# A fused recurrent attention and maxout layer on one core: another order of all its operations, 88 of them on other engines

## The chip, the cores and the metric

The kernel runs on one core of a Trainium2 chip. The metric is the device time of one execution in microseconds (us), as the median of several runs. The engines are named as in the profile: PE is TensorE (PEld its weight loads), DVE is VectorE, ACT is ScalarE, POOL is GpSimd, SP is SyncE, which issues all DMAs here.

## What is computed

The first half is a recurrence over 768 positions for 4 batches and 8 heads of 48 columns, the second a maxout layer on its output:

```python
for t in range(S):
    cur = einsum('bhd,bhe->bhde', u[None] * k[t], v[t])
    y[:, :, t] = einsum('bhd,bhde->bhe', r[t], state + cur)
    state = w[t][:, :, :, None] * state + einsum('bhd,bhe->bhde', k[t], v[t])
...
h1 = x @ w1                # x: y as 3072 tokens x 384;  w1, w2: 384 x 1024
h2 = x @ w2
out = maximum(h1, h2) @ w_out          # w_out: 1024 x 384
```

All inputs and the output are float32.

## The kernel before

The recurrence is worked in chunks of 256 positions, two positions to a partition (index i). Inside a chunk, decays are products of w, taken as prefix sums of logarithms; the products of r and k become matmuls, and a mask keeps the pairs of positions that may see each other. The 3 chunks of 4 batches are spread over eight *units*: units 0 to 3 are one batch of the first chunk each, unit 4 is batches 0 and 1 of the second chunk, unit 5 batches 2 and 3 of it, units 6 and 7 the same of the last chunk. Units of two batches have most operations once per batch (b) or twice as long. The maxout is folded: max(h1, h2) = relu(h1 - h2) + h2, so the kernel needs w1 - w2 (`wd_sb`), w_out (`wo_sb`) and w2 @ w_out (`wc_sb`).

Each operation has a short name with the unit first, then the batch or a group number. `@p`, `@d`, `@a` give the engine: POOL, DVE, ACT. What they do, with the line under which the profile shows them:

- `load.n.x` (L372): one of k, r, v, w of unit n from HBM into `lk`, `lr`, `lv`, `lw` (for some, into `wso`). `wload`, `woload`: the weights (`gT`, `wst` and `wso` as staging).
- `wp` (`lg`): product of two neighbouring w; `ln` (L387): its logarithm; `hi`, `lo` (L200, L202, L413): its split into two half-precision parts; `ex` (L398, or L395 and L396): prefix sum on PE; `mz` (L440, `MZ`): prefix sum plus the own term; `e0` (L436, in place in PSUM tile `G`) and `ie` (L460, `iE`): exponentials of the two.
- `rk`, `ru` (`rku`): r x k, times u; `dg` (L502): its row sums; `dd` (`gd`): a copy of them; `di` (L516): puts them on the diagonal of the mask tile `M`.
- `rw`, `kw`: r and k times the neighbouring w; `scale` (`rp`, `kp`): r and k times the exponentials; `vb` (`vp`): v in bfloat16.
- `tr` and `te` (L565, `RK`): transposes of rp and kp on PE and their copy; in units 5 to 7 `dt` (L582) instead, a transposing DMA.
- `kv` (L596): the state's update on PE; `st.n.0` (L612, `S_f`) and `st.n.1` (L615, `T`): added to the state; `sm` (`S_f<-T,W`): times the decay; `sb` (`S_b`): its copies in bfloat16.
- `sc` (L641): scores; `mk` (L650): masked copy of them from PSUM into `M`; `ya` (L688) and `yi` (L675): output from the scores and from the state, in one PSUM tile; `xe` (`xT`): its copy in bfloat16.
- `gt` (L706): x @ (w1 - w2), one of the groups of 512 columns; `rl` (L717 on ACT, L719 on DVE): relu; `op` (L725 and L729): output of one group of 128 tokens, 3 and 8 matmuls; `oe` (`osb`, `wb`): its copy; `os` (L743): its store.
- `hot` (L234): eight matmuls whose result is not used.

What sets the order is one list of these names, ORDER. Each engine does its operations in the order of that list, and SP issues the DMAs in that order too; an operation waits for its data and for the buffer that it writes. PSUM has four one-bank buffers `G` (prefix sums, transposes, `gt`, `op`, `hot`) and two two-bank buffers `Y` (`kv`, `sc`, and the output tile of `ya` and `yi`).

```python
for o in ORDER:
    o, _, e = o.partition("@")
    name, *a = o.split(".")
    a = [int(x) if x.isdigit() else x for x in a] + ([e] if e else [])
    if name in ops:
        ops[name](*a)
    else:
        unit[name](U[a[0]], *a[1:])
```

The engine letter chooses who does the operation. A product of 768 columns is done by DVE in one instruction and by POOL in two halves:

```python
def by_two(e, op, o, a, b):
    ...
    if e == "d" or n < 2 * HD:
        op(o, a, b)
    else:
        m = o.shape[1] // 2
        for g in (slice(0, m), slice(m, 2 * m)):
            op(o[:, g], a[:, g], b[:, g])
```

Of the kernel before, what the change touches and what calls it, by code (L numbers as in the profile page):

```python
# [54 lines left out]
load.0.w.1 load.0.w.0 wp.0.0@d hot.8.2 hot.8.3 load.2.w.0 zero.v.1@d wp.0.1@d mask ln.0.0 tri  # L55
zero.k.1@p load.1.w.0 ln.0.1 ex.0.0 load.1.r kw.0.0@d mz.0.0 wp.2.0@d rw.0.0@d load.1.k zero.o@p
load.0.v ie.0.0 uspread utake@a wp.1.0@d ex.0.1 ln.1.0 wload.1.0 mz.0.1 scale.0.1.0.0@p hot.8.0
zero.M.1@p ie.0.1 load.3.w.0 ru.0.0@d dg.0 rw.0.1@p kw.0.1@p scale.0.1.0.1@p wt.0.0 ex.1.0 we.0.0
e0.0.0 e0.0.1 wt.0.1 rk.1.0@d hot.8.5 vb.0.1@p load.2.r zero.v.2@d load.2.k load.1.v mz.1.0 ie.1.0
rw.1.0@d wt.1.0 wload.1.2 ln.2.0 ex.2.0 vb.0.0@a we.0.1 scale.0.0.0.0@d zero.k.0@d kv.0  # L60
scale.0.0.0.1@d tr.0.0.1 dd.0@p mz.2.0 woload.0 we.1.0 ru.1.0@p kw.1.0@p row.2 w2turn.0.0 e0.1.0
scale.1.0.0.0@d st.0.0@a tr.0.0.0 te.0.0.1@a sc.0.0.1.1 sc.0.0.0.1 w2turn.0.1 dg.1 te.0.0.0@a
w2take.0.0@a wload.0.2 load.2.v scale.1.1.0.0@d dd.1@p sb.0.0@a wp.3.0@p tr.1.0.1 e0.2.0 st.0.1
te.1.0.1@a rk.2.0@d zero.M.2@p di.0.0@d ie.2.0 zero.M.0@p rw.2.0@d hot.8.1 wload.1.1 ru.2.0@d
kw.2.0@p scale.2.1.0.0@p sc.0.0.1.0 sc.0.0.0.0 mk.0.0.1.0 vb.1.0@a hot.8.4 mk.0.0.0.0 mk.0.0.1.1
# [6 lines left out]
wocast.1@p gt.1.1 w2take.1.1@d woload.3 gt.0.0 rw.3.0@p woload.2 rl.0.0@a gt.1.2 load.4.w.0 rl.1.2@a
vb.2.0@p ru.3.0@p gt.0.3 rl.0.3@a ex.3.0 wocast.3@d wocast.2@a wocast.0@a rl.1.1@a di.2.0@d
sc.2.0.1.0 mk.2.0.1.0 gt.0.1 mz.3.0 e0.3.0 kw.3.0@p gt.1.0 dg.3 sc.2.0.0.0 kv.2 st.2.0@a rl.0.1@a
wp.4.0@d ie.3.0 scale.3.0.0.0@d mk.2.0.0.0 wfold.2 sb.2.1@d wfold.0 dd.3@p ln.4.0 load.3.v st.2.1
wfold.1 sb.2.0@d vb.3.0@a wl.2 hi.4@a lo.4@d ya.2.0.0.0 load.4.r rl.1.0@a di.3.0@d vb.3.1@a row.3
ya.2.0.1.0 wctake.1@a we.2 load.4.k wctake.2@a rk.4.0@d wctake.0@a scale.3.1.0.0@p tr.3.0.0 ex.4.0
mz.4.0 tr.3.0.1 ex.4.1 mz.4.1 te.3.0.0@a kv.3 te.3.0.1@a st.3.0@a yi.2.0 xe.2.0@d ie.4.0 op.1.1
oe.1.1@a st.3.1 load.4.v e0.4.0 sb.3.0@a ru.4.0@d gt.2.0 load.5.w.0 rl.2.0@a sc.3.0.0.0 sc.3.0.1.0
vb.4.1@a gt.2.2 op.1.0 rk.4.1@p rw.4.0@d kw.4.0@d scale.4.0.0.0@d scale.4.1.1.0@d scale.4.1.0.0@p  # L80
e0.4.1 rl.2.2@a scale.4.0.1.0@d op.0.1 sb.3.1@a row.4 oe.1.0@a tr.4.1.0 te.4.1.0@a tr.4.1.1 vb.4.0@a
op.0.0 sm.2@p wl.3 mk.3.0.0.0 ya.3.0.0.0 mk.3.0.1.0 ya.3.0.1.0 yi.3.0 oe.0.1@d ru.4.1@p wp.5.0@p
we.3 sm.3@p te.4.1.1@a gt.2.1 xe.3.0@a dg.4 ln.5.0 oe.0.0@d tr.4.0.1 te.4.0.1@a gt.3.0 rl.3.0@a
rl.2.1@a hi.5@a dd.4@d load.5.k kv.4 di.4.0@d sc.4.1.1.0 load.5.r load.5.v rk.5.0@d gt.2.3 rl.2.3@a
gt.3.2 tr.4.0.0 di.4.1@d te.4.0.0@a mk.4.1.1.0 gt.3.3 st.4.0 st.4.1 os.1.0 rl.3.3@a gt.3.1 rl.3.1@a
ru.5.0@p sc.4.1.0.0 rk.5.1@p sc.4.0.0.0 load.6.r sb.4.0@a vb.5.1@a op.2.1 load.6.w.0 lo.5@d wl.4
ex.5.0 mk.4.0.0.0 os.0.0 sb.4.1@a mk.4.1.0.0 oe.2.1@a mz.5.0 e0.5.0 rw.5.0@p ex.5.1 sc.4.0.1.0
load.6.k ru.5.1@p mz.5.1 ya.4.0.0.0 scale.5.0.0.0@d op.2.0 rl.3.2@a op.3.0 mk.4.0.1.0 e0.5.1 os.1.1
scale.5.0.1.0@d dt.5.0.0 ya.4.0.1.0 dt.5.0.1 kw.5.0@d row.5 oe.3.0@d os.3.0 wp.6.0@p ie.5.0
# [24 lines left out]
""".split()


# [681 lines left out]
```

## Time and profile before

| what | value |
|---|---|
| median of 3 runs | 146.66 us (146.49 to 146.94) |
| profiled execution | span 147.2 us, which is its own time here |
| mean granted PE clock | 0.987 |
| HBM read, written | 23.61 MB, 4.73 MB |

The page names time, engine, operation and the tiles written and read. In the list of waits a row has who waited, for whom, the total in us, the number of times and the longest. In a timeline a row has start, length, engine, line, operation, tiles, count, and in brackets the idle time of the engine just before and what ended it. In the groups, the first number after the bar is the busy time in us, the second the mean length in ns; then the idle time before. In the stretches, each engine has its busy time and number of instructions, PEclk is the granted share of PE's clock. The chain of work that ended last gives start, length and what stood on it.

### The profile page before, as it was taken

To read this page: it belongs to the slowest core of one execution; us is meant where nothing else is said; L and a number is where in the kernel's file an instruction comes from. 1 tells how busy PE (TensorE), PEld (TensorE's weight loads), DVE (VectorE), ACT (ScalarE), POOL (GpSimd) and SP (SyncE) were. 2 spreads that over 40 slices of the span, in tenths; PEclk is the share of its full clock that TensorE was granted. 3 is DMA by queue.
4 is the path that set the end of the run, shared out by engine and by line. 5 is a ranking of instruction groups with operands and counts; after the bars stand their busy time and mean duration, and the time that the engine had idled before them with its cause. 6 is when DMAs were issued, how large, how long until landed. Compare 5 with 4: busy or idle time off the path is not lost.

```text
span 147.2 us, 5536 instructions
## 1 busy us (share of the span) xinstructions
PE 136.8 (93%) x2403; PEld 84.2 (57%) x2404; DVE 116.9 (79%) x162; ACT 90.6 (62%) x164; POOL 90.0 (61%) x106
## 2 busy tenths in 40 slices
...
DVE  2489999999999999999999967399967589361511
...
PEclk9999999999999999999999999599999999999999
...
GB/s 104 323 325 357 335 401 394 366 286 304 214 241 277 212 226 282 312 255 174 205 192 177 292 251 207 141 138 291 250 136 78 131 271 20 0 210 62 4 56 157
DMA packets 71186, 31.84 MB, mean 216 GB/s; under 512 B 66293, under 2 KB 70390, under 8 KB 71162
## 3 DMA queue, kind: packets, MB, share of 16 engines
...
q14 instruction: 5, 0.04, 0.2%
HBM read 23.61 MB, written 4.73 MB: 193 GB/s over the span
## 4 chain that ended last, share of the span: by engine, by line
PE 41%; DVE 35%; issue 6%; POOL 6%; DMA 4%; ACT 3%; SPq 2%; DVEq 0%; POOLq 0%; ACTq 0%
PE G L729 12%; DVE M L650 9%; PE G L706 8%; PE G L234 7%; PE G L725 5%; DVE rp L176 4%; DMA lv<-in_v_dram 4%; DVE rku L176 3%; DVE dg L502 3%; POOL kp L180 3%; DVE M L516 3%; PE Y L688 2%; SPq L582 2%; POOL rku L180 2%; PE Y L675 2%
## 5 line engine op out<-in xcount | busy, mean ns | idle before, releaser
L729 PE MATMUL G<-wo_sb,gT 128*128 128x384 bf16 x192 | 35.8, 331 | 0.0
L706 PE MATMUL G<-xT,wd_sb 128*128 128x256 bf16 (+1 forms) x192 | 34.4, 326 | 0.7 <-ACT xT L168 0.6
L650 DVE CAST_PREDICATED M<-mask,Y 128x1024 bf16<-128x1024 int32 (+1 forms) x26 | 28.6, 1131 | 2.8 <-PE Y L641 1.9
L717 ACT ACTIVATE gT<-G 128x512 bf16<-128x512 f32 x43 | 24.5, 601 | 9.8 <-PE G L706 9.6
L729 PEld LDWEIGHTS <-gT 128*128 128x128 bf16 x192 | 19.0, 99 | 12.6 <-issue 0.3
L706 PEld LDWEIGHTS <-wd_sb 128*128 128x128 bf16 x192 | 17.9, 98 | 12.6 <-DVE wd_sb L176 0.6
L180 POOL TENSOR_TENSOR kp<-lk,iE 128x384 bf16<-128x384 f32 x16 | 17.1, 1096 | 9.3 <-DVE lk L176 4.2
L725 PE MATMUL G<-wc_sb,xT 128*128 128x384 bf16 x72 | 15.7, 327 | 0.0
L180 POOL TENSOR_TENSOR rku<-rku,u_b 128x384 f32<-128x384 f32 x14 | 14.5, 1053 | 2.0 <-DVE rku L176 2.0
L234 PE MATMUL G<-S_b 128*128 128x512 bf16 x47 | 13.6, 442 | 1.8 <-DVE S_b L263 1.8
L168 ACT COPY RK<-G 128x1024 bf16<-128x1024 bf16 x12 | 12.1, 1019 | 4.7 <-PE G L565 4.7
L168 ACT COPY osb<-G 128x384 f32<-128x384 f32 x7 | 3.4, 479 | 15.9 <-PE G L729 12.6
L180 POOL TENSOR_TENSOR rku<-lr,lk 128x384 f32<-128x384 f32 x8 | 10.9, 1393 | 2.5 <-DMA lk<-in_k_dram 1.7
L641 PE MATMUL Y<-RK 48*64 48x128 bf16 x384 | 9.0, 220 | 2.6 <-DVE M L650 2.4
L502 DVE TENSOR_REDUCE dg<-rku 128x16 f32<-128x768 f32 x12 | 11.0, 945 | 0.1
L641 PEld LDWEIGHTS <-RK 48*64 48x64 bf16 x384 | 6.2, 106 | 7.8 <-issue 6.7
L168 ACT CAST xT<-Y 128x768 bf16<-128x768 f32 x7 | 7.0, 1025 | 5.3 <-PE Y L675 4.0
L168 ACT CAST S_b<-S_f 64x768 bf16<-64x768 f32 (+1 forms) x14 | 8.7, 624 | 2.3 <-DVE S_f L612 2.0
L176 DVE TENSOR_TENSOR rp<-lr,G 128x768 bf16<-128x768 f32 (+2 forms) x11 | 8.8, 799 | 1.4 <-ACT G L436 1.4
L234 PEld LDWEIGHTS <-S_b 128*128 128x128 bf16 x48 | 5.1, 112 | 8.3 <-issue 3.3
L516 DVE TENSOR_TENSOR M<-identq,gd 128x512 int32<-128x512 int32 x12 | 9.2, 778 | 0.4 <-POOL gd L168 0.3
L168 DVE CAST xT<-Y 128x768 bf16<-128x768 f32 x5 | 5.1, 1017 | 5.5 <-PE Y L688 3.2
...
## 6 DMA issues: line engine op xcount, KB each, us to landing
...
```

The lines of the kernel that those rows point to most:

```text
L168: (nc.scalar.copy if e == "a" else nc.vector.tensor_copy if e == "d" else nc.gpsimd.tensor_copy)(o, i)
L176: op(o, a, b)
L180: op(o[:, g], a[:, g], b[:, g])
L234: nc.tensor.matmul(t, zz[:, 0:P], zz[:, 0:512], start=True, stop=True)
L502: nc.vector.reduce_sum(s.dg[:, b].rearrange("p i h -> p h i"), s.rku[:, b], axis=AX.X)
L516: (nc.vector if en == "d" else nc.gpsimd).tensor_tensor(out=o, in0=m, in1=g.unsqueeze(3).to_broadcast([P, 2, H, Q // 2]), op=ALU.bitwise_and)
L641: nc.tensor.matmul(t[q * Q:(q + 1) * Q, e, p * P:(p + 1) * P].rearrange("s (i g) -> s i g", i=2), s.kT[d, b, j, y * n + p, q, :], s.rT[d, ...
L650: nc.vector.copy_predicated(t[:, :, 2 * n * y:2 * n * (y + 1)].rearrange("s i (p e) g -> s p e i g", e=2), mask[:, j].bitcast(I32).unsquee ...
L706: nc.tensor.matmul(t[:, m * n * P:(m + 1) * n * P].rearrange("c (b t) -> c b t", t=P), wd_sb[:, ko, fo * P:(fo + 1) * P], s.xT[:, 0:n, ko, :],
L717: nc.scalar.activation(o, i, AF.Relu)
L725: nc.tensor.matmul(t[:, 0:HD], s.xT[:, a, ko, :], wc_sb[:, ko, :], start=(ko == 0), stop=False)
L729: nc.tensor.matmul(t[:, 0:HD], s.gT[:, c:c + P], wo_sb[:, f, :], start=False, stop=(f == FO - 1))
```

## The change

Only the list ORDER is changed. It has the same 652 operations in another order, and 88 of them have another engine letter: 27 from POOL to DVE, 19 from DVE to POOL, 20 from DVE to ACT, 15 from ACT to DVE, 5 from POOL to ACT, 2 from ACT to POOL. Of the loads, those of unit 0 begin with v instead of k.

```diff
 ORDER = """
-ident zero.s.1@p identq@a load.0.k load.0.r zero.m@p identb@p u zero.s.0@d zero.r@d rk.0.0@d
...
+zero.v.0@p ident zero.s.0@d zero.r@d hot.8.4 zero.s.1@p mask zero.o@p load.0.v vb.0.0@a zero.m@p
...
```

Three places of it, as the built programs have them. First DVE at the program's start, up to the first `mz` (`MZ`): before,

```order
L176 TENSOR_TENSOR rku<-lr,lk 128x768
L176 TENSOR_TENSOR lg<-lw 128x192
L254 MEMSET vp_77 128x8x2x8
L255 MEMSET vp_77 128x8x2x8
L176 TENSOR_TENSOR lg<-lw 128x192
L176 TENSOR_TENSOR lw<-lk,lw 128x4x48
L440 TENSOR_TENSOR MZ<-G,lg 128x4x48
```

and after the change:

```order
L176 TENSOR_TENSOR lg<-lw 128x192
L168 CAST identb<-osb 128x128
L168 COPY MZ<-osb 128x1
L440 TENSOR_TENSOR MZ<-G,lg 128x4x48 x2
L257 MEMSET M_82 128x512
L176 TENSOR_TENSOR lw<-lr,lw 128x4x48
```

The first `rku`, the memsets of `vp`, the second half of `lg` and the product of k and w have moved behind `MZ` or to POOL.

Second, DVE around unit 5's state sums and masks (`S_f` and `T` are `st.5.0` and `st.5.1`, the masked copies are `mk`): before,

```order
L650 COPY_PREDICATED M_80<-mask,Y 128x8x2x64
L612 TENSOR_TENSOR S_f<-Y,S_f 128x384
L650 COPY_PREDICATED M_80<-mask,Y 128x8x2x64
L615 TENSOR_TENSOR T<-Y,S_f 128x384
L440 TENSOR_TENSOR MZ<-G,lg 128x8x48 x2
L176 TENSOR_TENSOR lk<-lk,lw 128x16x48
L516 TENSOR_TENSOR M_81<-identq,gd 128x2x256
```

and after the change:

```order
L516 TENSOR_TENSOR M_81<-identq,gd 128x2x256
L176 TENSOR_TENSOR rku<-lr,lk 128x768
L612 TENSOR_TENSOR S_f<-Y,S_f 128x384
L176 TENSOR_TENSOR rku<-lr,lk 128x768
L615 TENSOR_TENSOR T<-Y,S_f 128x384
L650 COPY_PREDICATED M_80<-mask,Y 128x8x2x64 x2
L440 TENSOR_TENSOR MZ<-G,lg 128x8x48 x2
```

Both masked copies of batch 0 now stand behind `T`, with two products `rku` of unit 6 between. On PE, `sc.5.0.0.0` (the second score group of unit 5) now writes the `Y` buffer that `T` reads last; before, it wrote the one that the first masked copy reads.

Third, SP's DMAs around the transposes of unit 5 (`RK`) and the load of v of unit 6 (`lv`): before,

```order
L582 DMA_TRANSPOSE RK<-rp_73 128x8x128 x2
L472 DMA row<-MZ 1x1024
L743 DMA out_dram<-osb 128x384
L743 DMA out_dram<-wb 128x384
L582 DMA_TRANSPOSE RK<-kp_75 128x8x128 x2
L372 DMA lv<-in_v_dram 128x8x96 x2
```

and after the change:

```order
L582 DMA_TRANSPOSE RK<-kp_75 128x8x128
L472 DMA row<-MZ 1x1024
L743 DMA out_dram<-osb 128x384
L582 DMA_TRANSPOSE RK<-kp_75 128x8x128
L582 DMA_TRANSPOSE RK<-rp_73 128x8x128
L372 DMA lv<-in_v_dram 128x8x96 x2
```

The two `kp` that these transposes read were written by POOL before (`scale.5.1.0.0@p`, `scale.5.1.1.0@p`) and are written by DVE now; one store is no longer ahead of the load.

More of the change, by code (lines that the diff above doesn't have):

```diff
@@ L53 @@
 ORDER = """
-ident zero.s.1@p identq@a load.0.k load.0.r zero.m@p identb@p u zero.s.0@d zero.r@d rk.0.0@d
[L55 to L65, printed above, removed]
@@ L72 @@
[L72 to L83, printed above, removed]
@@ L84 @@
[L84 to L89, printed above, removed]
@@ new lines @@
+tr.1.0.1 sc.0.0.0.0 mz.2.0 ie.2.0 wload.0.0 kv.1 tr.1.0.0 load.3.r mk.0.0.0.0 st.1.0@a load.3.k
+row.2 st.1.1 te.1.0.1@a sb.1.0@a w2take.1.1@d sm.1@p di.1.0@d sc.0.0.0.1 mk.0.0.0.1 w2turn.0.0
+w2take.0.0@a e0.2.0 w2turn.0.1 w2turn.2.1 te.1.0.0@a w2take.0.1@a wocast.1@a wocast.2@a sc.0.0.1.1
+dg.2 ya.0.0.0.1 ya.0.0.1.0 rw.2.0@p yi.0.0 scale.2.0.0.0@d mk.0.0.1.1 w2turn.2.0 ya.0.0.0.0
+ya.0.0.1.1 xe.0.0@a w2take.2.0@a kw.2.0@p sc.1.0.1.0 wocast.0@p wfold.0 load.2.v wctake.0@a
+wdiff.1@d scale.2.1.0.0@d tr.2.0.0 mk.1.0.1.0 sc.1.0.0.0 sm.0@p mk.1.0.0.0 te.2.0.0@a sb.1.1@a
@@ new lines @@
+rl.0.2@a ya.2.0.0.0 di.3.0@d hi.4@a ya.2.0.1.0 xe.2.0@a scale.3.1.0.0@p kv.3 tr.3.0.0 oe.1.1@a
+tr.3.0.1 te.3.0.1@a lo.4@d op.1.0 st.3.0@d sb.3.1@a sb.3.0@a te.3.0.0@a st.3.1 ex.4.0 rk.4.0@d
+rk.4.1@d rw.4.0@d row.3 ex.4.1 mz.4.1 mz.4.0 oe.1.0@a load.4.v gt.2.3 sc.3.0.1.0 rl.2.3@a ie.4.0
+e0.4.0 e0.4.1 vb.4.0@a sc.3.0.0.0 gt.2.2 mk.3.0.1.0 mk.3.0.0.0 op.0.0 load.5.w.0 wl.3 yi.3.0
+ya.3.0.0.0 oe.0.0@a rl.2.2@a ya.3.0.1.0 load.5.r zero.v.2@p xe.3.0@a kw.4.0@p scale.4.1.1.0@d
+scale.4.0.1.0@d gt.2.1 rl.2.1@a scale.4.0.0.0@d gt.2.0 tr.4.1.1 ru.4.1@p tr.4.1.0 ru.4.0@d dg.4
@@ new lines @@
+dd.4@d gt.3.1 rl.2.0@a di.4.0@d op.2.1 scale.4.1.0.0@p te.4.1.1@a wl.2 vb.4.1@a kv.4 load.5.k we.2
+te.4.1.0@a sc.4.1.1.0 rl.3.1@a gt.3.0 op.0.1 sm.2@d we.3 wp.5.0@p ln.5.0 sm.3@p st.4.0 sb.4.0@a
+hi.5@a tr.4.0.0 rk.5.0@p ru.5.0@p di.4.1@d mk.4.1.1.0 st.4.1 lo.5@d sc.4.1.0.0 sb.4.1@a yi.4.1
+rl.3.0@a oe.2.1@a tr.4.0.1 te.4.0.0@a te.4.0.1@a ex.5.0 ya.4.1.1.0 mk.4.1.0.0 oe.0.1@d ya.4.1.0.0
+row.4 xe.4.1@a rk.5.1@d load.6.w.0 wp.6.0@d gt.3.2 gt.3.3 sc.4.0.0.0 sc.4.0.1.0 rl.3.2@a ex.5.1
+rl.3.3@a op.3.1 mz.5.0 ln.6.0 e0.5.0 wl.4 op.3.0 hi.6@a mk.4.0.0.0 load.5.v os.0.0 load.6.r mz.5.1
```

71 lines of the change are left out of this document (41 added, 30 removed).

## The prediction

> **What bounds the kernel now.** I read the page first: busy time, the slices, the chain that ended last.
>
> ```profile
> span 147.2 us, 5536 instructions
> PE 136.8 (93%) x2403; PEld 84.2 (57%) x2404; DVE 116.9 (79%) x162; ACT 90.6 (62%) x164; POOL 90.0 (61%) x106
> DVE  2489999999999999999999967399967589361511
> PEclk9999999999999999999999999599999999999999
> GB/s 104 323 325 357 335 401 394 366 286 304 214 241 277 212 226 282 312 255 174 205 192 177 292 251 207 141 138 291 250 136 78 131 271 20 0 210 62 4 56 157
> PE 41%; DVE 35%; issue 6%; POOL 6%; DMA 4%; ACT 3%; SPq 2%; DVEq 0%; POOLq 0%; ACTq 0%
> ```
>
> TensorE and VectorE share the chain: VectorE is full from slice 4 to slice 23 (of 3.68 us each) and has holes later; TensorE looks full all along. Its busy time contains pipelined ends, so the waits tell more. They are few, in the list of who waited for whom:
>
> ```profile
> PE Y L641 <- DVE M L650: 2.4, 3, 1.9
> PE G L234 <- DVE S_b L263: 1.8, 1, 1.8
> PE G L565 <- DVE rp L176: 0.8, 2, 0.5
> ```
>
> The second is the start of the program. What is left to win on TensorE is small, and most of it stands in one place, which TensorE's timeline and the stretches around it show:
>
> ```profile
> 79.89 0.42 PE L641 MATMUL Y<-RK 48*64 48x128 bf16 x16 [0.27 <-DMA RK<-kp]
> 81.77 0.42 PE L641 MATMUL Y<-RK 48*64 48x128 bf16 x16 [0.17 <-DVE M L650]
> 82.12 0.82 PE L706 MATMUL G<-xT,wd_sb 128*128 128x512 bf16 x3
> 87.29 1.46 PE L729 MATMUL G<-wo_sb,gT 128*128 128x384 bf16 x8
> 90.70 0.42 PE L641 MATMUL Y<-RK 48*64 48x128 bf16 x16 [1.94 <-DVE M L650]
> 91.54 2.16 PE L729 MATMUL G<-wo_sb,gT 128*128 128x384 bf16 x8
> 123.48 0.42 PE L641 MATMUL Y<-RK 48*64 48x128 bf16 x16 [0.24 <-DVE M L650]
> ...
> core 0: us, PE busy (x) PEld busy (x) DVE busy (x) ACT busy (x) POOL busy (x), PEclk, DMA share, GB/s
> 88.73:92.15 3.42, 1.48 (x24) 1.01 (x24) 2.90 (x3) 2.19 (x4) 3.42 (x5) 1.00 0.86 189
> 92.15:95.57 3.42, 3.42 (x100) 2.01 (x99) 1.13 (x3) 1.22 (x2) 1.85 (x2) 0.50 0.76 145
> 23.90:27.30 3.40, 2.50 (x59) 1.88 (x58) 3.40 (x6) 1.59 (x3) 3.32 (x4) 1.00 1.04 398
> ```
>
> TensorE stands still for 1.94 us at 88.76, is busy for only 1.48 us of the stretch of 3.42 us around that, and in the next 3.42 us it is granted half its clock: the same eight matmuls take 2.16 us instead of 1.46. So one late mask costs 1.94 us of waiting and 3.42 / 2 = 1.71 us of slow clock. The chain tells why it came late:
>
> ```profile
> 79.96 6.14 DMA lv<-in_v_dram
> 86.17 0.04 ACT vp L168
> 86.91 0.47 ACT G L436
> 88.55 0.95 DVE rp L176
> 89.51 1.15 DVE M L650
> ```
>
> The load of v of unit 6 was issued behind the transposes of kp (unit 5), which waited for GpSimd's scalings; ScalarE then stood at the cast of v, and behind it the exponential that VectorE's rp needs.
>
> **The change part by part.** 88 operations change engine: 27 go from GpSimd to VectorE, 19 back, 20 from VectorE to ScalarE, 15 back, 7 from either of GpSimd and ScalarE to the other. Priced by the groups by shape:
>
> ```profile
> L180 POOL TENSOR_TENSOR rku<-lr,lk 128x384 f32<-128x384 f32 x8 | 10.9, 1393 | 2.5 <-DMA lk<-in_k_dram 1.7 <-POOL gd L168 0.8
> L180 POOL TENSOR_TENSOR kp<-lk,iE 128x384 bf16<-128x384 f32 x16 | 17.1, 1096 | 9.3 <-DVE lk L176 4.2 <-ACT iE L460 3.9 <-issue 1.1
> L176 DVE TENSOR_TENSOR rku<-lr,lk 128x768 f32<-128x768 f32 x6 | 6.4, 1062 | 3.5 <-DMA lr<-in_r_dram 3.5
> L176 DVE TENSOR_TENSOR kp<-lk,iE 128x768 bf16<-128x768 f32 x2 | 2.2, 1108 | 0.1
> L168 DVE CAST xT<-Y 128x768 bf16<-128x768 f32 x5 | 5.1, 1017 | 5.5 <-PE Y L688 3.2 <-PE Y L675 2.3
> L168 ACT CAST xT<-Y 128x768 bf16<-128x768 f32 x7 | 7.0, 1025 | 5.3 <-PE Y L675 4.0 <-PE Y L688 1.3
> ```
>
> A full product costs GpSimd two halves (2 x 1.39 for rku, 2 x 1.10 for kp) and VectorE 1.06 and 1.11 once. Summed over all moves so, GpSimd loses 14.7 us, ScalarE gains 5.7, VectorE gains 2.9. GpSimd's saving is off the path except where kp was late. VectorE's gain is not, so I follow VectorE.
>
> *Its start.* Both kernels put 16 warm-up matmuls (L234) ahead of the first prefix sum, so VectorE's first MZ cannot start before the 8.25 us that it has now.
>
> ```profile
> 5.50 0.96 DVE L176 TENSOR_TENSOR rku<-lr,lk 128x768 f32<-128x768 f32 x1 [3.49 <-DMA lr<-in_r_dram]
> 8.25 0.36 DVE L440 TENSOR_TENSOR MZ<-G,lg 128x192 f32<-128x192 f32 x1 [0.48 <-PE G L398]
> 83.37 0.55 DVE L615 TENSOR_TENSOR T<-Y,S_f 128x384 f32<-128x384 f32 x1
> ```
>
> Between 5.50 and 8.25 VectorE now does six things (0.96 + 0.36 + 0.17 + 0.17 + 0.30 + 0.35 = 2.3 us by their rows); in the new order only one half of lg and the two small identity copies (0.6) are left there, since v, w and r are loaded ahead of k. So 1.7 us of work is pushed behind the first MZ. The loads themselves hide: k is then the fifth load, 1.54 MB into the queue, and by the GB/s row (104 and 323 over slices of 3.68 us) 1.57 MB have moved by 7.4 us; VectorE wants it at about 10.5.
>
> *Up to the second state sum of unit 5 (T, L615, 83.92 at its end).* From there the lists compare cleanly. Ahead of it come 27 operations from other engines, 19.7 us: five rku products or scalings (5.0), four kp scalings (4.3), wp of units 3 and 6 (1.9), the difference of weights (1.4), the rest small. Ahead of it go 26, 17.7 us: xT of three groups (3.0), wp, kw and rk of units 2, 4 and 5 (5.8), three osb copies (1.6) and so on. The two masks of unit 5, batch 0, are now behind it (2.4) and one diagonal ahead (0.7). Sum: +0.3. With 1.7 of the start, and 0.5 where the rp scaling of unit 5 meets an exponential that ScalarE reaches later (ScalarE has more to do from 50 us on), T ends at 83.9 + 2.5 = 86.4.
>
> Who waits for that: the score matmuls of unit 5, batch 0, second half, now take the PSUM buffer that T empties (now: the one that the first mask empties, the wait of 0.17 at 81.77). TensorE has done the same list of work at 82.9 in the trace (the end of the gate matmuls of 82.12). So it is 3.5 us late there, part in small waits for masks and buffers from 45 us on (about 1.5), the rest, some 2.0, in one wait at T.
>
> VectorE could also be earlier. Its operations stretch where GpSimd works beside it:
>
> ```profile
> L516 DVE TENSOR_TENSOR M<-identq,gd x12: 676/684/1497, 21.3 to 123.3; 128x512 int32<-128x512 int32 x12
> ```
>
> The same diagonal takes 0.68 or up to 1.50. [...] A sixth of GpSimd's work goes (14.7 of 90.0). The stretching in VectorE's rku group is 6.4 - 6 x 0.96 = 0.6 us, a tenth of it; on all of VectorE's 116.9 us that would be 11, of which a sixth is 1.8. So 0 to 1.8 us may come back, and I take 0.5, since the early products, where the lists stay mixed, keep their neighbours. The term is 3.5 - 0.5 = +3.0; its ends are +1.7 (all of the 1.8) and +4.5 (nothing comes back, and one more wait of 1 us like the one for the exponential).
>
> *After it.* Scalings of kp of unit 5 on VectorE let the transposes and the load of v go without GpSimd, and the exponential stands ahead of the cast of v on ScalarE. The wait of 1.94 goes, with it the slow clock, 1.71, and the 0.24 at 123.48 (those at 79.89 and 81.77 are inside the 82.9 above). What is late next is VectorE itself, which reaches unit 5's last mask with the same work ahead (92.9 against 93.0 us), 1.7 later less the 1.9 that it idles there now:
>
> ```profile
> 88.55 0.95 DVE L176 TENSOR_TENSOR rp<-lr,G 128x768 bf16<-128x768 f32 x1 [1.37 <-ACT G L436]
> 91.16 1.22 DVE L650 CAST_PREDICATED M<-mask,Y 128x1024 bf16<-128x1024 int32 x1 [0.52 <-PE Y L641]
> ```
>
> From there to the last mask it has 3.2 us more than now, but it idles more than that in this part (slices 30 to 33 read 6758: 1.4 slices or 5.2 us), so TensorE is the limit. Sum: -3.9, ends -2.2 (the clock is lost elsewhere) and -4.3 (the waits of 0.27 and 0.17 go as well).
>
> *The end.* Behind the last mask stand eight gate matmuls and five outputs as before, with relu split four to four instead of five to three; output is copied by ScalarE (0.48) instead of VectorE (0.56). -0.1, taken as 0; no load is left in the queue there.
>
> Sum: +3.0 - 3.9 = -0.9 on the profiled execution, whose own time is its span, 147.2; the median of the runs is 146.66, 0.5 lower. Forecast 145.8.
>
> **The rivals.**
> *The new wait also halves the clock (slower).* The stall at T is 2 us long and TensorE is busy before and after. If 1.94 us of it fall into one stretch of the clock's 3.42, the case in the trace repeats: +1.7, so 147.5. For: the row of 88.73, where 43% of busy time was too little. Against: 74% was enough at 23.90 (the clock stays at 9 in every slice but the 26th), and the stall may straddle two stretches. It decides from where the idle share of a stretch passes some point between 26% and 57%. [...]
>
> *VectorE keeps up.* If GpSimd's relief is the whole 1.8 and the pushed work of the start finds gaps later, T ends at about its old time; the small waits from 45 us on go with it. With +0.5 left of the term, 0.5 - 3.9 gives -3.4: 143.3. Against: no gap on VectorE above 0.5 us between 8.3 and 86 in which pushed work could hide.
>
> *More waits than a walk along two engines finds (slower).* ScalarE has 5.7 us more in its list. In the new order a copy of xT of unit 4 and the casts of v stand ahead of relus whose PSUM buffers TensorE wants next; one such wait is 0.5 to 1, three of them 2 to 3: 148.5 to 149.5. One copy of an output (group 4.0) now also shares its buffer with the store before it (4.2). For: casts of xT of 1.0 us at the head of that list. Against: ScalarE is 62% busy, so it catches up soon. It decides from where such a wait outlasts what TensorE has left in its four PSUM buffers, which no row shows.
>
> **How the numbers follow.** A change under 0.3%, 0.44 us, cannot be told from none here. Chances: the sum as it stands 0.38 (144.8 to 146.9, a quarter of it inside the 0.44, the rest faster), clock halved at the new place 0.27 (a quarter inside, the rest slower), VectorE keeps up 0.19, more waits 0.16. That is faster 0.28 + 0.19 = 0.47, same 0.10 + 0.07 = 0.17, slower 0.20 + 0.16 = 0.36. The range leaves out a tenth at each end: 143.0 to 149.3.
>
> **What would show it.** In the new profile: VectorE's first rku well behind 8 us (start); a wait of TensorE at L641 of about 2 us near 84 to 87, released by VectorE's L615 (the price); no wait of 1.94 and full clock between 88 and 96 (the gain); VectorE's holes after 97 smaller. Wrong would make it: waits of TensorE spread over 40 to 80 that ScalarE ends, a second stretch at 0.50, or no wait at L615.

## The result: 2.7% slower, and the profile after

The changed kernel takes 150.54 us (median of four runs, 149.89 to 151.59), the kernel before 146.80 beside it (146.49 to 147.06): a ratio of 1.0271, 95% interval 1.0223 to 1.0319. The forecast was 145.8.

A run's time is its span and 1.7 to 1.9 us more, so a median of 146.66 belongs to a span of about 144.9, and the profiled execution of before that the prediction read (span 147.2, clock 0.987) was of a rare kind: of 80 further runs of that kernel three had spans of 147.3 to 148.1 at a clock of 0.988, one 146.6, and the others 144.1 to 145.9.

The page of after, in the order of the lines shown of before (size, busy time, slices, DMA rates, chain):

```profile
span 148.2 us, 5530 instructions
PE 136.5 (92%) x2404; PEld 84.1 (57%) x2404; DVE 119.2 (80%) x165; ACT 96.1 (65%) x172; POOL 80.8 (55%) x92
DVE  2189999999999999999999899898599587545110
PEclk9999959999999999999999999999999999999999
GB/s 106 300 278 335 348 371 375 389 306 247 298 273 275 231 249 280 49 107 253 330 168 219 200 179 326 176 239 285 184 166 66 174 160 4 106 111 215 4 106 106
PE 45%; DVE 22%; SPq 13%; DMA 8%; POOL 5%; issue 4%; ACT 0%; DVEq 0%
```

GpSimd lost 9.2 us of its 90.0 (less than the priced 14.7), VectorE and ScalarE gained 2.3 and 5.5. VectorE is now full from slice 4 to slice 22, with two short dips behind. The loads have a hole of two slices near 60 us (49 and 107 GB/s). The half clock (0.50) has moved to 19.1 to 22.5 us. Little of its price shows, because the same kernel run again at full clock waits there instead (0.6 us for ScalarE and 0.8 for VectorE between 21.9 and 24.6 us). The list of TensorE's waits, as for before:

```profile
PE Y L688 <- issue: 1.8, 1, 1.8
PE Y L641 <- DMA RK<-kp: 0.9, 1, 0.9
PE G L565 <- DVE kp L176: 0.8, 1, 0.8
PE G L706 <- DVE rp L176: 0.7, 1, 0.7
```

The wait for masks (`PE Y L641 <- DVE M`) is gone. In its place stand many waits of less than 1 us, and one of 1.8 us at L688 with no releaser ("issue": nothing that the profile shows was waited for). Rows of the timelines of after, VectorE and then TensorE, at the places that the prediction named:

```profile
7.94 0.62 DVE L440 TENSOR_TENSOR MZ<-G,lg 128x192 f32<-128x192 f32 x2 [0.96 <-PE G L398]
11.02 0.90 DVE L176 TENSOR_TENSOR rku<-lr,lk 128x768 f32<-128x768 f32 x1
84.04 0.55 DVE L615 TENSOR_TENSOR T<-Y,S_f 128x384 f32<-128x384 f32 x1
...
84.55 0.64 PE L641 MATMUL Y<-RK 48*64 48x128 bf16 x32
108.29 0.94 PE L688 MATMUL Y<-M,vp 64*32 64x128 bf16 x84
111.06 0.57 PE L688 MATMUL Y<-M,vp 64*32 64x128 bf16 x44 [1.83 <-issue]
```

`T` ends at 84.59 and the scores behind it begin without a wait. At 108.3, 84 of the 128 matmuls of `ya` run; the other 44 follow 1.83 us later.

To see where the time went, I count TensorE's operations with the duration that each has when nothing holds it (0.65 us for a gate group, 1.80 for an output of 11 matmuls, 0.14 or 0.25 for a score group and so on: 122.4 us in all). What TensorE's time exceeds that sum by, up to the same amount of work, is lost time (us):

| work done | near | before, as predicted from | before, again | after | after, again |
|---|---|---|---|---|---|
| 20 | 29 us | 9.1 | 8.8 | 9.4 | 10.0 |
| 40 | 52 us | 11.9 | 11.7 | 12.7 | 13.2 |
| 60 | 75 us | 13.4 | 13.1 | 15.9 | 17.0 |
| 70 | 85 us | 14.7 | 14.4 | 16.5 | 17.5 |
| 85 | 103 us | 19.5 | 16.8 | 18.8 | 19.6 |
| 95 | 116 us | 20.1 | 17.4 | 21.8 | 22.5 |
| all | end | 21.7 | 19.0 | 22.6 | 23.3 |

The first column is some 0.3 too high throughout, since one warm-up matmul (L234) is missing from that trace (2403 records, 2404 in the others). Against the usual before, after loses 3.6 to 4.3 us: 0.6 to 1.2 by 29 us, 2.2 to 2.7 more by 75; it wins 0.8 to 1.1 back by 103, loses 2.3 to 2.4 more by 116, and wins 0.8 back by the end.

### The profile page after: what moved, and what is told of

Read it like the earlier page. It is cut to its first block, busy times and chain, and to the rows that moved or that the text cites. A ratio compares the mean times of both kernels' runs of the same rounds, so it can differ in the third digit from the quotient of the medians.

```text
span 148.2 us, 5530 instructions
## 1 busy us (share of the span) xinstructions
PE 136.5 (92%) x2404; PEld 84.1 (57%) x2404; DVE 119.2 (80%) x165; ACT 96.1 (65%) x172; POOL 80.8 (55%) x92
## 4 chain that ended last, share of the span: by engine, by line
PE 45%; DVE 22%; SPq 13%; DMA 8%; POOL 5%; issue 4%; ACT 0%; DVEq 0%
PE G L706 15%; PE G L729 14%; DVE M L650 7%; SPq L372 7%; PE G L725 6%; DMA lw<-in_w_dram 5%; SPq L285 4%; DMA RK<-kp 3%; POOL rku L180 3%; PE Y L688 3%; DVE rku L176 2%; DVE kp L176 2%; PE Y L641 2%; SPq L290 2%; PE Y L596 2%
## 5 line engine op out<-in xcount | busy, mean ns | idle before, releaser
L717 ACT ACTIVATE gT<-G 128x512 bf16<-128x512 f32 x41 | 23.5, 598 | 14.0 <-PE G L706 13.8
L706 PEld LDWEIGHTS <-wd_sb 128*128 128x128 bf16 x192 | 17.9, 98 | 13.1 <-issue 1.4
L180 POOL TENSOR_TENSOR rku<-rku,u_b 128x384 f32<-128x384 f32 x14 | 15.9, 1153 | 0.0
L234 PE MATMUL G<-S_b 128*128 128x512 bf16 x48 | 13.9, 447 | 1.8 <-DVE S_b L263 1.8
L168 ACT CAST xT<-Y 128x768 bf16<-128x768 f32 x10 | 10.3, 1029 | 3.7 <-PE Y L688 2.6
L168 ACT CAST vp<-lv 128x768 bf16<-128x768 f32 (+1 forms) x13 | 9.2, 707 | 4.6 <-DMA lv<-in_v_dram 4.6
L180 POOL TENSOR_TENSOR kp<-lk,iE 128x384 bf16<-128x384 f32 x10 | 11.2, 1144 | 0.1
L688 PE MATMUL Y<-M,vp 64*32 64x128 bf16 x768 | 9.1, 219 | 2.2 <-issue 1.8
L180 POOL TENSOR_TENSOR rku<-lr,lk 128x384 f32<-128x384 f32 x6 | 6.6, 1127 | 7.1 <-DVE gT L719 5.2
L234 PEld LDWEIGHTS <-S_b 128*128 128x128 bf16 x48 | 5.2, 114 | 8.9 <-issue 4.1
L641 PE MATMUL Y<-RK 48*64 48x128 bf16 x384 | 9.2, 223 | 1.0 <-DMA RK<-kp 0.9
L516 DVE TENSOR_TENSOR M<-identq,gd 128x512 int32<-128x512 int32 x12 | 9.7, 813 | 0.6 <-ACT gd L168 0.5
L688 PEld LDWEIGHTS <-vp 64*32 64x32 bf16 x768 | 7.2, 90 | 5.0 <-issue 4.4
L168 ACT COPY osb<-G 128x384 f32<-128x384 f32 x11 | 5.3, 478 | 7.2 <-PE G L729 7.1
L168 ACT CAST S_b<-S_f 64x192 bf16<-64x192 f32 (+1 forms) x16 | 9.4, 588 | 0.6 <-DVE S_f L612 0.4
```

Of the source, the lines that this page charges most:

```text
L168: (nc.scalar.copy if e == "a" else nc.vector.tensor_copy if e == "d" else nc.gpsimd.tensor_copy)(o, i)
L234: nc.tensor.matmul(t, zz[:, 0:P], zz[:, 0:512], start=True, stop=True)
L641: nc.tensor.matmul(t[q * Q:(q + 1) * Q, e, p * P:(p + 1) * P].rearrange("s (i g) -> s i g", i=2), s.kT[d, b, j, y * n + p, q, :], s.rT[d, ...
L688: nc.tensor.matmul(lhsT=s.vp[g, b, 2 * p + e, j, m * 32:(m + 1) * 32], rhs=s.M[b, j][g, :, 2 * p + e, :], **into(s, b, q, p * 96 + (e + m) ...
L706: nc.tensor.matmul(t[:, m * n * P:(m + 1) * n * P].rearrange("c (b t) -> c b t", t=P), wd_sb[:, ko, fo * P:(fo + 1) * P], s.xT[:, 0:n, ko, :],
L717: nc.scalar.activation(o, i, AF.Relu)
```

## The experiments

**The kernel before again.** Nothing is changed.

> The kernel before, unchanged, run and profiled again. Theory P (the profiled execution that the prediction read was longer than the usual ones, by a mask that came late once): span 144.5 to 145.5, time 146.5 to 147, no wait of TensorE of 1.9 us near 89 and full clock near 92. Theory Q (that execution was typical): the wait of 1.9 us and the half clock appear again, span about 147. If P holds, the 3.9 us that the prediction booked as a gain were never in the time to be beaten.

146.40 us, ten runs of 146.13 to 146.66. Its page:

```profile
span 144.7 us, 5537 instructions
PEclk9999999999999999999999999999999999999999
```

TensorE's timeline at the place of the wait:

```profile
89.66 0.42 PE L641 MATMUL Y<-RK 48*64 48x128 bf16 x16 [0.94 <-DVE M L650]
```

and the stretch around it:

```profile
88.42:91.84 3.42, 2.48 (x29) 1.35 (x27) 2.90 (x4) 1.45 (x4) 3.42 (x4) 1.00 1.04 217
```

The wait is 0.94 instead of 1.94, its stretch is 73% busy instead of 43%, and the clock stays. Theory P holds: TensorE's last matmul ends at 141.41 here and at 143.83 in the execution that was read, so 2.4 us of what was to be won was in that one execution and not in the time to be beaten.

**Order and letters apart.** Two kernels: the order of before with the 88 letters of after, and the order of after with the letters of before.

> The order of before with the 88 engine letters of after. If the loss of 3.7 us lies in the order (loads and transposes late in SP's queue, the start), this runs within 1 us of before: 146 to 148. If it lies in the letters (5.7 us more on ScalarE, 2.9 more on VectorE), it takes about what after takes, 149.5 to 151.5. If the letters fit only the order that was sought with them, it is slower than both, over 152.

> The order of after with the engine letters of before. Loss in the order: 149.5 to 151.5 as after. Loss in the letters: 146 to 148. Letters and order fitted to each other: over 152.

169.25 us (1.1496, 1.1432 to 1.156) and 168.27 (1.1496, 1.1444 to 1.1547). The third theory: letters and order fit only each other, and neither is good or bad by itself. The sum of prices by letter, with which the prediction began, says little about such a list.

**The changed kernel again.**

> The changed kernel, unchanged, run and profiled again. If its losses are built into the list (waits behind WL in SP's queue near 57 to 63, late transposes of unit 6 at 105, half clock near 21, a stop of 1.8 us without a releaser at 109), they stand at the same places again, span 148 to 149.8. If they are chance, other places show them and the span may come down to 146.

149.89 us (149.69 to 150.61), at full clock. The losses stand at the same places; rows of TensorE's timeline:

```profile
57.15 0.74 PE L688 MATMUL Y<-M,vp 64*32 64x128 bf16 x64 [0.68 <-DVE M L650]
59.38 0.82 PE L706 MATMUL G<-xT,wd_sb 128*128 128x256 bf16 x6 [0.72 <-DVE rp L176]
111.78 0.57 PE L688 MATMUL Y<-M,vp 64*32 64x128 bf16 x44 [1.75 <-issue]
```

So they are built into the list, and the stop without a releaser falls on the same matmul.

**An output between the small matmuls.**

```diff
-ya.6.1.1.0 ya.6.1.0.0 ya.6.0.0.0 ya.6.0.1.0 ... dt.7.0.0 op.5.3 op.5.2
+ya.6.1.1.0 ya.6.1.0.0 op.5.3 ya.6.0.0.0 ya.6.0.1.0 ... dt.7.0.0 op.5.2
```

> After, with one entry of the list moved: op.5.3 (11 matmuls of 128x384, 1.8 us) stands between ya.6.1.0.0 and ya.6.0.0.0 instead of four entries later. Theory I: the stop of 1.8 us of TensorE in ya.6.0.0.0 is a wait for its own instructions: a transfer of 16 KB on the instruction queue begins there at 109.5, and the dense ya matmuls (84 of them in 0.94 us) use up what is left before it lands; 11 slow matmuls bridge it. Then the stop goes and the run takes 1.5 to 2.0 us less than after: 148.0 to 148.5. Rival D: the stop is a wait for data (a masked copy, vp) that the trace does not name; then it stays behind op.5.3, and 0 to 0.3 us are won. Rival M: the stop moves to the next dense run (sc.7, ya.7): 0 won.

149.51 us (148.24 to 150.42; 1.0188, 1.0145 to 1.0232). In the trace the stop at `ya` is gone: the two halves of `ya` stand at 108.74 and 111.62 with `op.5.3` between (it waits 0.26 us for `osb`), and neither waits. But 0.5 us of a wait without a releaser appears at `kv.7`, 6 us on. The median is 0.4 below that of the repeated after, less than the spread of either. The place is confirmed, the price is not.

**Three operations off VectorE.**

```diff
-rk.4.1@d rw.3.0@d wctake.1@d
+rk.4.1@p rw.3.0@p wctake.1@a
```

> After, with rk.4.1 and rw.3.0 back from VectorE to GpSimd and wctake.1 from VectorE to ScalarE: 2.05 us less on VectorE ahead of the masks of unit 3. Theory V: TensorE's waits between 54 and 60 (0.85 at yi.3.0 for a mask, 0.90 at gt.2.1 for rp) come from VectorE's list, which has no gap from 9 to 86 us; they go, and 1.0 to 1.8 us are won: 148.1 to 148.9. Rival G: GpSimd's rk.4.1 (about 2.8 us) makes kw and kp of unit 4 late, the transposes wait instead, and the time stays within 0.4 of after or gets worse.

150.51 us (149.60 to 151.53; 1.0275, 1.0233 to 1.0317): the rival's time, but not its cause. The wait for the mask shrank from 0.68 to 0.35, the one for `rp` stayed (0.73), and the transposes of unit 4 behind it do not wait. What ate the gain in this trace is a new wait of 1.6 us for `xT` on VectorE, up to 98 us.

**Two buffers for WL.**

```diff
-s.WL = tile_of(s, [P, 2 * NP], F32, "WL", 1)[:, s.x * NP:(s.x + s.nb) * NP]
+s.WL = tile_of(s, [P, 2 * NP], F32, "WL", 2)[:, s.x * NP:(s.x + s.nb) * NP]
```

> After, with two buffers for WL instead of one, so that the load wl.4 need not wait for the exponentials we.2 and we.3, and SP does not stand at it between 56 and 63 us with the loads of units 5 and 6 behind it. Theory S: the hole in the loads (45 to 81 GB/s in two slices) makes v, r and k of units 5 to 7 late, and with them the last transposes and masks: 0.5 to 1.5 us won, 148.4 to 149.4. Rival H: the hole is hidden, because TensorE's waits grow by only 0.4 us between 60 and 82 us: within 0.3 of after, 149.6 to 150.2.

150.01 us (148.56 to 152.40; 1.0215, 1.0175 to 1.0256). The rates of slices 17 to 21 are 226, 283, 248, 80 and 84 instead of 49, 107, 253, 330 and 168: the hole is only moved, and the time did not change clear of the spread. The hole is hidden, as rival H said.

**An earlier copy on ScalarE.**

```diff
-vb.1.1@a ... ln.2.0 sb.0.0@a e0.1.0 we.1.0 w2take.1.0@a
+w2take.1.0@a vb.1.1@a ... ln.2.0 sb.0.0@a e0.1.0 we.1.0
```

> After, with w2take.1.0 (ScalarE's copy that frees a PSUM buffer) ahead of five other ScalarE operations instead of behind them, so that ex.2.0 at 22.6 need not wait 1.2 us for a buffer. If TensorE's waits at the start count by themselves, 0.8 to 1.2 us are won: 148.7 to 149.1. Rival: VectorE is full from 9 to 86 us, so TensorE, earlier here, waits the same time more at the masks of 54 to 60 us: 0 to 0.3 won, 149.6 to 149.9.

149.45 us (148.47 to 153.91; 1.0192, 1.0147 to 1.0237). The wait for ScalarE's buffer (0.63 us in the repeated after) is gone. Behind it TensorE waits longer for `rp` on VectorE (1.03 us in two waits instead of 0.83), and the mask wait of 57 us shrinks from 0.68 to 0.17. So in this trace TensorE is 0.6 us ahead of the repeated after at 28 us and 1.1 at 59, but level with the first trace of after (58.27 and 58.31 for the same gate matmuls). The median lies between the two expectations and within the spread: neither is shown.

**Halves of the two lists joined.** Before up to `yi.4.0` (73 us) and after behind it; the same with `op.5.3` between; and the opposite join.

> Two lists joined behind yi.4.0 (TensorE's last operation of unit 4's recurrence, at 73 us before): ahead of it order and letters of before, behind it those of after (op.3.1, ln.6.0, hi.6, we.4 stand at the seam). In the first part after loses about 2.7 us of TensorE's time to before (waits for VectorE from 14 to 30 and from 54 to 72 us), in the second it wins 2.0 (no wait for the masks of unit 5) and loses 2.0 (the stop of 1.8 in ya.6.0.0.0) and 0.4 (late transposes). Theory (the losses add, part by part): 146.5 + 0.4 = 146.6 to 147.4, if the stop is there with 1 to 1.8 us. Rival (the parts are tied by buffers and by VectorE's queue, as the order and the letters were): over 148.5.

> The joined list with op.5.3 between ya.6.1.0.0 and ya.6.0.0.0 too. Theory I (the stop is a wait for instructions in a dense run of small matmuls): 1.0 to 1.8 us less than the joined list without it, 145.0 to 146.2, so faster than before. Rival (the stop only changes place): the same as without it.

> The opposite join: after up to yi.4.0, before behind it. Theory (losses add): 146.5 + 2.7 = 148.5 to 149.8, with TensorE 2.5 to 3.5 us behind at yi.4.0 and full work from there. Rival (VectorE, late by the first part, finds slack behind it, since before has gaps there from 87 us on): 147 to 148.

149.63 us (148.02 to 149.85), 149.30 (147.95 to 150.27) and 151.97 (151.07 to 153.04); ratios 1.0202 (1.0159 to 1.0245), 1.018 (1.0136 to 1.0224), 1.0378 (1.0331 to 1.0424). The joins made waits of their own. In the first two ScalarE copies `xT` of unit 4 too late, and TensorE waits 2.2 us. What the prediction's first rival describes, half the clock behind such a wait, is in one of their two profiles. TensorE's timeline behind the wait in the first join:

```profile
77.61 2.75 PE L706 MATMUL G<-xT,wd_sb 128*128 128x512 bf16 x12 [2.22 <-ACT xT L168]
```

in the second:

```profile
77.53 4.44 PE L706 MATMUL G<-xT,wd_sb 128*128 128x512 bf16 x12 [2.21 <-ACT xT L168]
```

and the stretch behind the wait in the second (PEclk, third from the end, is 0.51; in the first join it is 1.00 throughout):

```profile
78.00:81.40 3.40, 3.40 (x10) 1.27 (x9) 2.28 (x3) 0.36 (x1) 0.00 (x0) 0.51 1.21 278
```

Behind the same wait at the same place the clock is halved in one execution and not in the other: the twelve matmuls take 4.44 us instead of 2.75. Of the first join's six runs the one at clock 1.00 has a span of 146.2, the five at 0.986 to 0.988 have 147.7 to 148.0, so 1.5 to 1.8 us more, near the 1.71 that the prediction gave one halved stretch. The second join's six runs divide in the same way: one at 0.999 with 146.2, five at 0.985 to 0.989 with 147.4 to 148.6. Where the clock falls was seen only in the one profile; that it is this place in the other runs is inferred from clock and span. What decides between the two is not shown.

The opposite join waits 2.4 us for masks (L641) and 1.2 us for `xT`. It is slower than the theory allowed, so the half of before does not run behind that of after as it does behind its own.

**Two copies and one scaling of before moved.**

```diff
-oe.3.0@d oe.2.0@d ... scale.6.0.0.0@d ... mk.5.1.0.0
+oe.3.0@a oe.2.0@a ... mk.5.1.0.0 scale.6.0.0.0@d
```

> Before, with the output copies oe.3.0 and oe.2.0 (0.55 us each) on ScalarE, which is idle from 70.3 to 73.7, instead of VectorE, and scale.6.0.0.0 behind mk.5.1.0.0 on VectorE. It asks whether before's own waits for the masks of unit 5 (0.68 and 1.10 us at 80 to 89) can be had without the new order. Theory: VectorE reaches those masks 1.0 to 2.0 us earlier and 0.9 to 1.7 us are won: 144.9 to 145.7. Rival: the next thing that VectorE needs (an exponential on ScalarE, behind the cast of v) is no earlier, and 0 to 0.4 are won.

145.43 us (eleven runs, 144.99 to 145.95; 0.9934, 0.9913 to 0.9956): 0.7% faster than before, little but clear of the spread. VectorE's timeline of the usual before, then the timelines of VectorE and of TensorE here:

```profile
88.39 1.22 DVE L650 CAST_PREDICATED M<-mask,Y 128x1024 bf16<-128x1024 int32 x1
...
87.24 1.21 DVE L650 CAST_PREDICATED M<-mask,Y 128x1024 bf16<-128x1024 int32 x1
...
88.82 0.42 PE L641 MATMUL Y<-RK 48*64 48x128 bf16 x16
```

The mask starts at 87.24 instead of 88.39, because the scaling that waited 0.36 us for ScalarE's exponential now stands behind it, and TensorE's wait of 0.94 is gone. The copies won nothing that shows: `T` ends at 84.06, and at 83.89 in before. What the usual runs have of the wait at 88 us goes, by these rows, when one operation is moved.

**The join mended.** `xe.4.0` ahead of `ln.6.0`; the same with `op.5.3` between; and with the two copies as well.

> The joined list (before up to yi.4.0, after behind it) with xe.4.0 ahead of ln.6.0 on ScalarE, so that TensorE need not wait 2.4 us at the seam for xT of unit 4, and the clock is not halved behind it (granted 0.986 to 0.988 in five of six runs of the first join). Theory (parts add): span 143.8 to 144.8, time 145.6 to 146.6, the stop in ya.6.0.0.0 still there. Rival (the seam's wait hid others on VectorE): over 147.5.

> The mended join with op.5.3 between ya.6.1.0.0 and ya.6.0.0.0. Theory I (the stop is a wait for instructions): 0.8 to 1.6 us less than the mended join, 144.4 to 145.4. Rival (it moves or turns into a wait for data): less than 0.4 of difference.

> The mended join with op.5.3 between and with the two copies oe.3.0 and oe.2.0 on ScalarE. If these help here as they did in before (0.9 us for two copies and one scaling), 143.8 to 145.0, less than any kernel so far (145.4). Rival: the new second half has no wait for the masks of unit 5 any more, so copies off VectorE are worth nothing: within 0.3 of the one without them.

146.40 (145.74 to 148.33; 0.9978, 0.9944 to 1.0013), 146.63 (146.02 to 148.91; 0.9991, 0.9961 to 1.0021) and 146.31 us (145.70 to 147.76; 0.9989, 0.9952 to 1.0026). With the first 73 us of before, the second half of after costs and wins nothing that can be measured, so the loss of 3.7 us comes with the first half and what follows from it. None of the three has the stop in `ya`; the second half was not measured behind this first half with the stop in it. The outcome of `op.5.3` could not be measured here, since the stop was not there in the first place. TensorE's timeline in the first of the three:

```profile
106.31 1.38 PE L688 MATMUL Y<-M,vp 64*32 64x128 bf16 x128
```

All 128 matmuls of `ya` run through. TensorE's order is the same as in the first join, where a stop of 1.00 us stood inside them: so the place in the list is not enough to make it. In the third a stop of 0.94 us without a releaser appeared elsewhere, at the transposes of unit 4 (63.4 us).

**The start.** `rk.0.0` and `zero.k.1` back to GpSimd.

```diff
-zero.k.1@d ... rk.0.0@d
+zero.k.1@p ... rk.0.0@p
```

> After, with rk.0.0 and zero.k.1 (0.95 + 0.3 us) from VectorE back to GpSimd, which is idle from 9.5 to 13.2. If the work pushed behind VectorE's first MZ is what makes the masks and scalings late up to 60 us (the prediction's second step), all of these come 1.0 to 1.3 us earlier, TensorE wins that at the transposes from 16 to 33 us, and the run takes 148.5 to 149.2. Rival: other work on VectorE's list fills the time (longer products beside GpSimd, waits for loads): 149.6 to 150.5 as after.

151.50 us (150.56 to 152.22; 1.0307, 1.0257 to 1.0357): slower than either expectation. The timelines of VectorE and GpSimd here:

```profile
10.34 1.09 DVE L176 TENSOR_TENSOR lw<-lk,lw 128x192 f32<-128x192 f32 x1
11.53 0.97 DVE L176 TENSOR_TENSOR kp<-lw,iE 128x192 bf16<-128x192 f32 x1
...
10.22 2.06 POOL L180 TENSOR_TENSOR rku<-lr,lk 128x384 f32<-128x384 f32 x2
```

and VectorE's in the repeated after:

```profile
10.51 0.35 DVE L176 TENSOR_TENSOR lw<-lk,lw 128x192 f32<-128x192 f32 x1
10.96 0.36 DVE L176 TENSOR_TENSOR kp<-lw,iE 128x192 bf16<-128x192 f32 x1
```

Beside GpSimd's product the same two VectorE products take 1.09 and 0.97 us instead of 0.35 and 0.36: so of the 1.25 us taken off VectorE all is given back at once (1.35). The rival had named this cause, but by these rows VectorE is hardly worse off than before. What makes the run slower than after is not shown. Its trace has two things more: a wait of 1.6 us for `xT` on VectorE near 99 us, as with the three operations off VectorE, and a stretch of half clock at the start (0.50 from 13.55 to 16.97 us), which the page's row of the granted clock shows in the fourth and fifth slice:

```profile
PEclk9998799999999999999999999999999999999999
```

Five of the six runs have such a clock (0.986 to 0.989), but the one at full clock, 150.86, is not the fastest. Whether the work pushed behind the first `MZ` makes the later waits could not be told in this way.

**The load of v of unit 7 earlier.**

```diff
-load.7.k ... dt.6.1.0 op.5.1 dt.6.0.0 sc.6.0.0.0 mk.6.0.0.0 wl.5 load.7.v
+load.7.k load.7.v ... dt.6.1.0 op.5.1 dt.6.0.0 sc.6.0.0.0 mk.6.0.0.0 wl.5
```

> After, with the load of v of unit 7 issued right behind that of k of unit 7 (about 97 us) instead of behind the transposes of kp and rp of unit 6 (104 us). Theory F: the fetch of TensorE's instructions waits behind those 768 KB, which flow from 105 to 109; without them the fetch begins before 107, lands ahead of the dense ya matmuls, and the stop goes: 0.6 to 1.8 us won, 148.2 to 149.6, if the transposes of unit 6, now behind the load, come no later. Rival T: they come 1 to 2 us later, the masks of unit 6 with them, and the time stays at 149.6 to 150.6. Rival P: the fetch is set by TensorE's position alone, the stop stays at the same matmul.

151.94 us (149.98 to 152.30; 1.0369, 1.0335 to 1.0402). The profiled execution is the fastest of the six. The time goes the way of rival T and beyond its range, the stop follows theory F; TensorE's timeline:

```profile
107.39 0.64 PE L641 MATMUL Y<-RK 48*64 48x128 bf16 x32 [1.47 <-DMA RK<-rp]
111.09 0.57 PE L688 MATMUL Y<-M,vp 64*32 64x128 bf16 x44 [0.30 <-issue]
```

The transposes now wait behind the load and cost 1.47 us; the stop shrank to 0.30.

**The lists joined earlier**, behind `wctake.0` (44 us): before ahead, after behind.

> Joined lists, cut behind wctake.0 of before (about 44 us; the two lists have done nearly the same work there): order and letters of before ahead of it, after behind it. Theory (VectorE's lateness of the first 44 us is carried to the masks and scalings of 54 to 72 us): TensorE's 1.1 us of the start and most of the 2.5 us of 54 to 72 go, span 144.5 to 146.0, time 146.3 to 147.8. Rival (the order of units 3 and 4 itself makes those waits): only the 1.1 us go, 148.5 to 149.5.

148.29 us (146.94 to 149.31; 1.0105, 1.0062 to 1.0148), between the two expectations. Of TensorE's loss from 40 to 45 us of work (1.5 to 2.1 in after, none in before) about 0.5 is left; of that from 50 to 55 (1.2 in after, 0.4 in before) all 1.3 is left. By this the first is in the main lateness carried from the first 44 us, and the second belongs to the order of unit 4. But this trace also has no stop in `ya`:

```profile
107.63 1.29 PE L688 MATMUL Y<-M,vp 64*32 64x128 bf16 x128
```

TensorE is 0.7 and 1.5 us ahead of the two traces of after as `ya` begins (107.63 against 108.29 and 109.09; 0.8 was lost to ScalarE's `wc_sb` at the seam), 2.7 and 3.4 ahead behind it, and 2.1 and 2.8 at its last matmul. So about 1.4 us of the lead, half of it or more, is the missing stop, and not the first 44 us.

## Why the prediction was wrong

**The execution that it was read from: the step that failed first.** "The profiled execution, whose own time is its span, 147.2; the median of the runs is 146.66, 0.5 lower": the span belongs to a time of about 149, some 2.2 above the median; that a profile's span is the run's own time, as the table of before also says, is wrong here by 1.7 to 1.9. Spans and clocks like its own stand in three of 80 runs; the repeated run had 0.94 us of the wait and a full clock. With the rows of that repeated run the gain behind `T` would have been 0.94 + 0.24 = 1.2 instead of 3.9, and the forecast 146.8 + 3.0 - 1.2 = 148.6. The page had a warning, the clock of 0.987 beside a median that no run left by more than 0.3.

**The start: right.** The first rku of VectorE stands at 11.02, behind the first `MZ` at 7.94 (8.69 in the repeated run; that it cannot start before 8.25 did not hold). TensorE loses 0.6 to 1.2 us more than the usual before by 29 us.

**Up to T, +3.0 (ends +1.7, +4.5): size right, place wrong.** `T` ends at 84.6 and 85.7 in the two profiles, against 86.4. TensorE's extra loss at that point is 2.1 and 3.1 us against the usual before. But there is no wait of 2 us at L641 for `T`. TensorE came late to `T` itself, by small waits from 18 to 70 us for scalings, masks, copies and a load (the prediction had 1.5 of its 3.5 there). Those of 0.15 us and more, without the one at the program's start, add up to 3.6 and 5.0 us, against 2.8 before `T` in the usual before; what is left of the extra loss stands in shorter delays and, in the first profile, in the half clock at 21 us. VectorE ends half of them in the first profile and two thirds in the second, ScalarE most of the rest. So that the size of the term came out is luck in part.

**GpSimd's relief, -0.5: not seen.** A group of after by shape:

```profile
L176 DVE TENSOR_TENSOR kp<-lk,iE 128x768 bf16<-128x768 f32 x5 | 7.0, 1408 | 0.0
```

Five full scalings on VectorE cost 1.41 us each, where the prediction priced 1.11 by two of them: 1.5 us more in this group alone, against 0.07 us less in each rku product (0.99 for 1.06). The diagonals (L516), by which the prediction argued, take 0.81 on average instead of 0.78. GpSimd has fewer operations, but those that are left run beside VectorE's products: of the five scalings, three have GpSimd busy from end to end (2.02, 1.45 and 1.67 us, at 31.08, 55.95 and 110.79), the other two have it idle (1.82 for both, at 77.80). The 0 to 1.8 us were the author's estimate, from one row and one group of before; that the stretching goes down with GpSimd's busy time is not shown.

**After T, -3.9 (ends -2.2, -4.3): the step that failed most.** Behind 70 us of work the usual before loses 4.6 us and after 6.1 and 5.8, so the change is +1.2 to +1.5. Even the execution that was read loses only 7.0, 0.9 to 1.2 more than after. The waits and the slow clock went as predicted; two new losses came, which no step had: the stop of 1.8 us in `ya.6.0.0.0`, and 0.6 to 0.9 for the transposes of kp of unit 6.

**The tail, 0: nearly right.** From 100 us of work on, after loses 0.65 us and before 1.1, so after wins some 0.4 there.

**The sum.** By its own steps, with the base set right: +2.1 to +3.1 up to `T`, +1.2 to +1.5 behind it, together 3.6 to 4.3; the medians differ by 3.7. The third rival ("more waits") had the right sign and nearly the time, 148.5 to 149.5, but its cause was ScalarE's list. What the traces of after show is waits for VectorE more than for ScalarE, and the stop; that VectorE's list makes the first part is argued from who ended the waits, since neither attempt to shorten it won time. The second rival ("VectorE keeps up") was right that `T` could come early, and wrong that this would be a gain. The first did not occur at `T`; behind a wait of 2.2 us in the joins the clock was 0.51 in one profile and 1.00 in the other. That the idle share of one stretch decides this is the author's reading of two rows of before, and after speaks against it: its half clock (0.50 from 19.1 to 22.5 us) stands right behind 3.40 us that were 78% busy (2.65), where 74% left the clock whole in before.

**What the stop is.** The times fit theory I: the matmuls wait for their own instructions. No view names what they wait for, so this is an inference. In every trace with a stop, a packet of 16 KB on the instruction queue begins shortly before it. The DMA queues of after, for 0.1 us from 108.8 on (packets, MB, share of the engines):

```profile
q1 hardware_dynamic: 41, 0.04, 113.1%
q8 instruction: 1, 0.02, 57.6%
```

| run | packet begins | matmuls go on | between |
|---|---|---|---|
| after | 108.85 | 111.06 | 2.2 |
| after again | 109.52 | 111.78 | 2.3 |
| three off VectorE | 109.42 | 111.68 | 2.3 |
| two WL buffers | 107.29 | 109.50 | 2.2 |
| early w2take | 107.87 | 110.12 | 2.3 |
| first join | 106.67 | 109.11 | 2.4 |
| all that helped (at unit 4) | 61.13 | 63.41 | 2.3 |
| load of v earlier | 108.46 | 111.09 | 2.6 |
| output between (at `kv.7`) | 113.27 | 115.84 | 2.6 |
| new order, old letters | 125.07 | 127.25 | 2.2 |

Every trace has 19 such packets, and most pass without a stop. What tells the traces apart is the time that TensorE has left. In none of the 20 does it reach this place of its program (the 1885th matmul, inside `ya`) sooner than 2.2 us after the packet began. Two without a stop reach it just then (2.19 in the mended join, 2.21 with the first products back on GpSimd), the other ten 2.4 to 6.6 after.

In the mended join the packet began at 104.92, with the output ahead of `ya`, and nothing stopped. In the traces with a stop at `ya` the packet began within 1 us of the end of a flow of some 320 GB/s, the 768 KB of `load.7.v`; where that load was moved away, it began 0.5 us into the output ahead of `ya` (108.46). DMA rates over 102 to 111 us, in 40 equal slices, of after:

```profile
GB/s 315 269 155 65 27 17 241 289 277 288 151 291 200 5 2 5 21 64 70 233 311 326 328 323 323 321 328 321 333 362 428 239 68 0 9 7 14 14 14 0
```

and of the mended join:

```profile
GB/s 5 39 101 214 306 326 328 306 301 304 326 324 402 347 360 289 116 21 7 14 20 0 0 0 0 0 0 73 0 0 0 0 0 0 0 0 175 216 217 207
```

The flow ends near 109.3 in after and near 105.7 in the join, where the packet (104.92) also began within its last microsecond, but early enough. These times, and the one run that moved the load (a stop of 0.30 instead of 1.75 to 1.83), speak for theory F, that the packet waits for the load. Two traces speak against it as a rule. In the lists joined earlier the packet begins at 105.88, in the middle of the same load (some 300 GB/s from 104.9 to 107.8); and where the stop came at unit 4, loads flow on at some 300 GB/s for 1.2 us behind the packet's start at 61.13. So what sets the start of the packet stays open, and what happens inside the queues was not measured.

**What stays open.** Which operations of the first 44 us make VectorE late: one attempt to relieve it there backfired. What the stop costs in time: taking it away won 0.4 us in the median, within the spread, with a stop of 0.46 us elsewhere; between single traces it was 1.4 (the lists joined earlier). What sets the time at which the packet begins.
